# Attention, routed experts and a gated layer on one core: the attention loop in one reordered form, embedding norms on GpSimd, gates in four parts, queries a tile sooner

## The chip, the cores and the metric

One core of a Trainium2 chip runs the whole program. The metric is the device time of one execution in microseconds (us), lower is better. PE is TensorE, DVE is VectorE, ACT is ScalarE, POOL is GpSimd, SP is SyncE, which issues most of the DMAs.

## The reference

Three layers, one after the other: a gated linear attention with a state per head (4 batches, 8 heads, 768 steps, 40 channels), a layer of 8 experts of which each token takes the one with the largest logit, and a gated layer.

```python
for t in range(S):                                   # attention
    m_new = max(f_gate[t] + m, i_gate[t])
    f_stab, i_stab = exp(f_gate[t] + m - m_new), exp(i_gate[t] - m_new)
    C = f_stab * C + i_stab * outer(v[t], k[t])      # state, 40 x 40 per head
    n = f_stab * n + i_stab * k[t]
    y[t] = sigmoid(o_gate[t]) * (C @ q[t]) / max(abs(n . q[t]), 1)
x = y as 3072 tokens of 320 channels
logits = norm(x) @ norm(expert_emb).T / tau          # experts
out[mask_e] = softmax weight * (relu(x @ w1[e]) @ w2[e])
return (sigmoid(x @ w_gate) * (x @ w_val)) @ w_out   # gated layer
```

## The kernel before

The sequence is cut into 6 chunks of 128 steps, with 4 batches: 24 tiles, numbered i, chunk c = i // 4 and batch b = i % 4. Inside a tile the attention is a masked matrix product; between the chunks of a batch a state cst[b] is carried. The code is written in the order in which each engine gets its instructions (no scheduler moves them), and each engine works its list strictly in that order. So a step that waits holds all that stands behind it on the same engine.

The steps of one tile, with the line of the profile:

- `load_qk`, `load_kv` (L283, L288): SP's DMAs of queries and keys (six buffers) and of keys, values and output gates (five buffers).
- `st_S(i)` (L422): PE multiplies keys and queries into two PSUM banks (s_ps). DVE masks the first half into am (L441), ACT copies it to f16 as ah (L442); DVE masks the second half in place (L443), ACT copies it (L444); POOL subtracts al for the first half (L445), DVE al for the second half (L446). ah and al are the high and low part of one number.
- `st_V(i)`, `st_V2(i)`: POOL scales the values into vw (L409), ACT copies vh (L418), POOL subtracts vl (L419).
- `st_AV(i)` (L449): PE multiplies state with queries and ah, al with vh, vl into o_ps, always bank 4 in the loop.
- `post_ops(i)` (L492): three small DVE operations on den, the sigmoid of the output gate on ACT (L490), x0 on DVE (L518), then POOL's `gated`: x (L504) and a copy of its last 64 columns (L507).
- `st_U(i)` (L468): PE's update of the state into u_ps (bank 5), then cst[b]: two operations, one for each half of the heads; on ACT in chunk 0 (L483), on DVE later (L485).
- `st_XT(i)` (L525): PE transposes x, ACT copies it to xt (L531) and sums squares (L534), SP stores x to xs.
- `st_logit(i)` (L537): three small matmuls, and DVE's copy to raw, which the profile names rs (L545).
- `st_route(c)`, `st_rank(c)`: DVE's choice of the expert (rmax, sel), four small sums on POOL (run, L569), some small matmuls on PE, and nine DVE operations (pf, posf, bm, oh_p, ob, oh_b). Eight of the nine go to the list `sideq`, from which `side()` takes one at a time.

The gates are computed by six DVE operations over 32 lanes (`gate_ops`, two of them scans along the sequence) and two exps on ACT (`st_gexp`); `st_gates2` transposes them on PE. They come in three parts: chunk 0, chunk 1, and chunks 2 to 5 together (512 columns). ACT loads a function table whenever it changes between Exp and Sigmoid.

The order around the change is written by hand. Tiles 0 to 2 run in a prologue of their own, woven with 15 small DVE operations that normalise the expert embeddings (`emb_norm`, with `sqrt_ops`). Then a loop runs i from 3 to 19. One round of it holds: loads for tile i+4, XT(i-1), AV(i), post(i), U(i), the rank step in every fourth round, V2(i+1), S(i+3), V(i+2), logit(i-1), route in every fourth round. Tiles 20 to 23 follow in a tail that is woven with the first expert's weights; then come the experts and the gated layer, which the change leaves as they are.

Of the kernel before, what the change touches and what calls it, by code (L numbers as in the profile page):

```python
# [22 lines left out]
def kernel(  # L23
# [250 lines left out]
    def kpart(i):  # L274
        return kv[i % NKV][:, KO:VO].rearrange("p (h d) -> p h d", d=D)
# [28 lines left out]
    def emb_norm():  # L304
        esq = ap_.tile([NE, DM], F32, name="esq")
        en1 = ap_.tile([NE, 4], F32, name="en1")
        return [
            lambda: nc.scalar.activation(out=esq, in_=eb, func=AF.Square, accum_out=en1[:, 0:1])
        ] + sqrt_ops(ap_, en1[:, 1:2], en1[:, 0:1]) + [
            lambda: nc.vector.tensor_scalar(  # L310
                out=en1[:, 2:3], in0=en1[:, 1:2], scalar1=1e-6, scalar2=tb, op0=ALU.add, op1=ALU.mult
            ),
            lambda: nc.vector.reciprocal(en1[:, 3:4], en1[:, 2:3]),
            lambda: nc.vector.tensor_scalar_mul(eb, eb, en1[:, 3:4]),
        ]
# [152 lines left out]
    def st_U(i):  # L468
# [68 lines left out]
    def st_logit(i):  # L537
# [7 lines left out]
        nc.vector.tensor_copy(raw[:, i, :], lp[:, 0:NE])  # L545
# [9 lines left out]
    def st_rank(c):  # L555
# [14 lines left out]
        pf = bp.tile([P, B, NE], F32, tag="pf", name="pf")  # L570
# [108 lines left out]
    NAHEAD = 3  # L679
    sideq = []  # L680
# [9 lines left out]
    st_S(0, lambda: st_gates2(0, 1))  # L690
    def load(i):
        load_qk(i)
        load_kv(i)

    post = {}

    def early(i):
# [16 lines left out]
    st_V(2)
    st_S(2, lambda: (early(0), st_V2(1)))
    load(4)
    st_U(0)
    st_V2(2)
    st_V(3)
    st_gates2(1, 2)  # L720
    load_qk(6)
    st_sig(0)
    st_sig(1)
    post[0][5]()
    st_S(3, lambda: early(1))
    st_U(1)
    st_V2(3)
    side(2)
    post[1][5]()
    load(5)  # L730
    st_S(4, lambda: (st_XT(0), early(2), side(len(sideq))))
    st_sig(2)
    load_kv(6)
    post[2][5]()
    st_V(4)
    st_U(2)
    st_S(5, lambda: (st_XT(1), emb_T(), st_AV(3), st_post(3)))
    sideq += gate_ops(2 * L, S)
    GX = 5
    for i in range(3, NTILE - B):  # L740
        load(i + 4)
        if i > 3:
            st_XT(i - 1)
            st_AV(i)
            post = post_ops(i)
            if i == GX + 1:
                del post[3]
            weave(post)
        else:
            st_logit(0)  # L750
            st_XT(2)
# [10 lines left out]
        st_U(i)  # L762
        if i > B and i % B == 1:
            rk = st_rank(i // B - 1)
            rk.pop(0)()
            sideq += rk
# [1312 lines left out]
```

## Time and profile before

| | us |
|---|---|
| three runs | 765.41, 765.99, 767.67 |
| median | 765.99 |
| the profiled execution, its own time | 767.39 |
| its span, first to last instruction | 765.6 |
| attention loop with its prologue, read from DVE | 0 to about 132 |
| PE busy in the span | 730.9 (95%) |
| DVE, ACT, POOL busy in the span | 402.4, 363.9, 395.5 |

The profile shows one execution. A row of a group gives line, engine, operation, output and inputs, their shapes, how often it ran, its busy time and the mean of one in ns, and the idle time of the engine just ahead of it with what ended that idle time. A row of a timeline gives start and length in us. The granted clock (PEclk) is 1.00 where TensorE runs at 2.4 GHz and 0.50 where it runs at 1.2 GHz.

### The profile page before, as it was taken

What the parts mean: (1) busy time and instruction counts of PE and PEld (TensorE: products, weight loads), DVE (VectorE), ACT (ScalarE), POOL (GpSimd) and SP (SyncE); (2) the same over time, 40 slices, a digit from 0 to 9 for tenths busy, and PEclk for the clock granted to TensorE, in tenths of its full rate; (3) what the DMA queues carried; (4) which work ended last, traced back from release to release, by engine and by line L of the source; (5) the groups of instructions that cost most, each with busy time, mean ns of one, the idle gap of its engine ahead of it and who ended that gap; (6) DMA issues with size and microseconds to landing.
All of it is one profiled execution on the core that took longest, in us unless ns stands there. A gap on an engine that the chain in (4) does not pass through costs nothing. (4 is left out here: it accounts for less than half of the span.)

```text
span 765.6 us, 17594 instructions
## 1 busy us (share of the span) xinstructions
PE 730.9 (95%) x6861; PEld 656.2 (86%) x6861; DVE 402.4 (53%) x864; ACT 363.9 (48%) x829; POOL 395.5 (52%) x449
## 2 busy tenths in 40 slices
PE   7789999899999999999989999999999999999995
PEld 6689998789888889999878888888888888888884
DVE  7878888778579787755576664223212111111111
ACT  5756554545775556666354454333323333333222
POOL 6667777647576767787153223544324334334222
PEclk9899999689999999999999999999999999999998
DMA  7644864544545565553122320000000000000001
GB/s 247 172 148 131 248 198 135 168 128 136 162 137 155 147 194 176 166 168 92 35 55 78 84 58 32 36 22 15 2 2 36 1 2 36 2 1 36 2 1 39
DMA packets 39864, 70.46 MB, mean 92 GB/s; under 512 B 4818, under 2 KB 28460, under 8 KB 39772
## 3 DMA queue, kind: packets, MB, share of 16 engines
q1 hardware_dynamic: 36764, 59.61, 26.1%
q0 software_dynamic: 3008, 9.64, 3.8%
q8 instruction: 56, 0.92, 0.5%
q14 instruction: 36, 0.29, 0.1%
HBM read 60.55 MB, written 8.68 MB: 90 GB/s over the span
## 5 line engine op out<-in xcount | busy, mean ns | idle before, releaser
L1586 POOL TENSOR_TENSOR hl<-sgm,hh 128x512 fp32r<-128x512 f32 x71 | 94.9, 1342 | 228.1 <-ACT hh L1585 228.1
L1575 DVE TENSOR_TENSOR sgm<-v_ps,sgm 128x512 f32<-128x512 f32 (+1 forms) x73 | 49.7, 682 | 229.8 <-ACT sgm L1574 229.8
L1611 PE MATMUL o_ps<-wo,hl 64*128 64x320 f32 x560 | 87.2, 307 | 0.0
L1610 PE MATMUL o_ps<-wo,hh 64*128 64x320 f32 x560 | 86.7, 305 | 0.0
L1609 PE MATMUL o_ps<-wo,hh 64*128 64x320 f32 x560 | 86.3, 303 | 0.0
L1574 ACT ACTIVATE sgm<-g_ps 128x512 f32<-128x512 f32 (+1 forms) x73 | 43.2, 593 | 76.8 <-PE g_ps L1533 76.8
L1545 ACT COPY seen<-zeros 1x1 f32<-1x1 f32 x142 | 27.0, 190 | 109.1 <-PE v_ps L1533 61.5
L1585 ACT CAST hh<-sgm 128x512 fp32r<-128x512 f32 (+1 forms) x73 | 44.8, 615 | 47.9 <-DVE sgm L1575 47.6
L1014 ACT ACTIVATE hh<-h_ps 128x256 fp32r<-128x256 f32 (+7 forms) x72 | 35.2, 489 | 57.8 <-PE h_ps L926 54.8
L1531 PE MATMUL v_ps<-xg,wvh 64*128 64x512 f32 x144 | 56.5, 392 | 2.4 <-ACT seen L1545 2.4
L429 PE MATMUL s_ps<-qk 128*128 128x128 f32 (+1 forms) x384 | 54.4, 305 | 4.2 <-DMA qk<-in_qkt_dram 4.1
L1609 PEld LDWEIGHTS o_ps<-wo,hh 64*128 64x128 f32 x560 | 53.0, 185 | 6.3
L1610 PEld LDWEIGHTS o_ps<-wo,hh 64*128 64x128 f32 x560 | 52.8, 184 | 5.8
L1531 PE MATMUL g_ps<-xg,wgh 64*128 64x512 f32 x144 | 56.5, 392 | 0.0
L1532 PE MATMUL v_ps<-xg,wvh 64*128 64x512 f32 x144 | 56.4, 392 | 0.0
L1532 PE MATMUL g_ps<-xg,wgh 64*128 64x512 f32 x144 | 56.4, 392 | 0.0
L1532 PE MATMUL g_ps<-xl,wgh 64*128 64x512 f32 x144 | 56.4, 392 | 0.0
L1532 PE MATMUL v_ps<-xl,wvh 64*128 64x512 f32 x144 | 56.4, 392 | 0.0
L1531 PE MATMUL g_ps<-xh,wgh 64*128 64x512 f32 x144 | 56.3, 391 | 0.0
L1531 PE MATMUL v_ps<-xh,wvh 64*128 64x512 f32 x144 | 56.3, 391 | 0.0
L1533 PE MATMUL g_ps<-xg,wgl 64*128 64x512 f32 x144 | 56.2, 390 | 0.0
L1533 PE MATMUL v_ps<-xg,wvl 64*128 64x512 f32 x144 | 56.2, 390 | 0.0
(350 smaller groups left out, 2617.9 us busy)
## 6 DMA issues: line engine op xcount, KB each, us to landing
kv<-in_kvo_dram SPq DMA_DIRECT2D x24, 484.0 KB
w2raw<-in_moe_w_dram SPq DMA_DIRECT2D x32, 320.0 KB
w1raw<-in_moe_w_dram SPq DMA_DIRECT2D x32, 256.0 KB
qk<-in_qkt_dram SPq DMA_DIRECT2D x48, 160.0 KB
xs<-x SPq DMA_DIRECT2D x24, 192.0 KB
w1raw<-in_moe_w_dram SPq DMA_DIRECT2D x64, 64.0 KB
raw<-in_moe_w_out_dram SPq DMA_DIRECT2D x12, 320.0 KB
raw<-in_moe_w_gate_dram SPq DMA_DIRECT2D x8, 384.0 KB
```

The lines of the kernel that those rows point to most:

```text
L429: nc.tensor.matmul(pss[u][:, pr_ * L:(pr_ + 1) * L], qk[i % NQ][rows, 2 * u, pr_, :], qk[i % NQ][rows, 1, pr_, :], start=True, stop=True,)
L1014: nc.scalar.activation(out=h[f][0], in_=ps, func=AF.Relu)
L1531: lambda: nc.tensor.matmul(ps, at(wh), h[rows, kk], start=start, stop=False),
L1532: lambda: nc.tensor.matmul(ps, at(wh), l[rows, kk], start=False, stop=False),
L1533: lambda: nc.tensor.matmul(ps, at(wl), h[rows, kk], start=False, stop=stop),
L1574: nc.scalar.activation(out=s[:, cs], in_=pg[:, cs], func=AF.Sigmoid)
L1575: nc.vector.tensor_tensor(out=s[:, cs], in0=pv[:, cs], in1=s[:, cs], op=ALU.mult)
L1585: nc.scalar.copy(gh[:, cs], s[:, cs])
L1586: e.tensor_tensor(out=gl[:, cs], in0=s[:, cs], in1=gh[:, cs], op=ALU.subtract)
L1609: lambda: nc.tensor.matmul(o, gh[rows, ts_], wh[rows], start=begin, stop=False),
L1610: lambda: nc.tensor.matmul(o, gh[rows, ts_], wl[rows], start=False, stop=False),
L1611: lambda: nc.tensor.matmul(o, gl[rows, ts_], wh[rows], start=False, stop=end),
```

## The change

- The loop runs from i = 0 to 19; the prologue keeps only S of tiles 0 to 2 and what they need. A round now holds: queries of tile i+5 and keys and values of tile i+4, AV(i), XT(i-1), V2(i+1), post(i), U(i), S(i+3) with logit(i-1) inside, the rank step after it, V(i+2).
- The state update becomes one DVE operation for all heads into cc[b] (104 lanes, of which 24 hold nothing of use; the even heads' matmul writes 64 rows instead of 40), and two ACT copies from cc to cst. It stands inside S(i+3), between DVE's second masking and its subtraction.
- The logit copy goes from DVE to ACT for tiles below 20.
- The embedding norm computes its inverse root on POOL, with two DVE operations at its start and one near its end.
- The gates come in four parts: chunk 0, 1, 2, and 3 to 5 (384 columns).
- S of nine tiles (8, 10, 11, 13, 14, 16, 17, 19, 20) multiplies only the 40 rows that hold data, at partitions 0 and 64, instead of 128 rows with zeros; before, only tile 0 did.

The diff, cut to its core (the removed prologue of before, most of it, is the first "..." in the loop's part):

```diff
@@ emb_norm
+        step = [
+            lambda: two(t, y, sq, y, ALU.mult, ALU.mult),
+            lambda: two(t, t, -0.5, 1.5, ALU.mult, ALU.add),
+            lambda: g.tensor_tensor(out=y, in0=t, in1=y, op=ALU.mult),
+        ]
...
+        ] + 3 * step + [
+            lambda: g.tensor_tensor(out=y, in0=y, in1=sq, op=ALU.mult),
+            lambda: two(t, y, 1e-6, tb, ALU.add, ALU.mult),
+            lambda: v.reciprocal(r, t),
+            lambda: g.tensor_scalar_mul(eb, eb, r),
         ]
@@ st_S
-    def st_S(i, then=None):
+    def st_S(i, then=None, last=None):
...
-            rows = slice(0, P) if i else slice(DP * u, DP * u + D)
+            rows = slice(DP * u, DP * u + D) if i == 0 or i in HALF else slice(0, P)
...
+        aA[i] = (ah, al)
+        if last:
+            last()
         nc.vector.tensor_tensor(out=al[:, 1], in0=ps[1], in1=ah[:, 1], op=ALU.subtract)
-        aA[i] = (ah, al)
@@ st_U
-        for u in range(2):
-            sl = slice(DP * u, DP * u + D)
...
+        def add():
+            sl = slice(0, DP + D)
             pv = pu[sl, 0:NPR * DV].rearrange("p (a d) -> p a d", a=NPR)
             if c == 0:
-                nc.scalar.activation(out=cst[b][sl, :, u], in_=pv, func=AF.Copy, scale=SQ)
-                continue
-            nc.vector.scalar_tensor_tensor(
-                out=cst[b][sl, :, u], in0=pv, scalar=SQ, in1=cst[b][sl, :, u], op0=ALU.mult, op1=ALU.add
-            )
+                nc.vector.tensor_scalar_mul(cc[b][sl], pv, SQ)
+            else:
+                nc.vector.scalar_tensor_tensor(
+                    out=cc[b][sl], in0=pv, scalar=SQ, in1=cc[b][sl], op0=ALU.mult, op1=ALU.add
+                )
+            for u in range(2):
+                sl = slice(DP * u, DP * u + D)
+                nc.scalar.copy(cst[b][sl, :, u], cc[b][sl])
+
+        return add
@@ st_logit
-        nc.vector.tensor_copy(raw[:, i, :], lp[:, 0:NE])
+        (nc.scalar.copy if i < NTILE - B else nc.vector.tensor_copy)(raw[:, i, :], lp[:, 0:NE])
@@ prologue and loop
+    HALF = [i for i in range(8, NTILE - B + 1) if i % 3]
...
+    st_S(0, None, lambda: (st_gates2(0, 1), weave(ahead[0:2])))
+    weave(ahead[2:])
     st_V(0)
     st_V2(0)
+    norm = emb_norm()
+    weave(norm[0:7])
     st_gexp(L, 2 * L)
     st_S(1)
+    act_zero(qk[0])
     st_V(1)
+    weave(norm[7:])
+    st_S(2)
+    load_qk(4)
...
+    for i in range(NTILE - B):
+        if i + 5 < NTILE:
+            load_qk(i + 5)
+        load_kv(i + 4)
+        st_AV(i)
+        if i:
             st_XT(i - 1)
-            st_AV(i)
...
+        st_V2(i + 1)
+        post = post_ops(i)
+        if i in (G2 + 1, G3):
+            del post[3]
+        weave(post)
+        weave(scans.get(i, []))
...
-        st_U(i)
...
+        add = st_U(i)
...
-        st_S(i + NAHEAD, (lambda: st_logit(1)) if i == 3 else None)
+        def between():
+            add()
+            if i == 1:
+                emb_T()
+            if i:
+                st_logit(i - 1)
+
+        st_S(i + NAHEAD, None, between)
+        if i > B and i % B == 1:
+            rk = st_rank(i // B - 1)
...
+        if i == G2:
+            st_sig(i + 1)
+            st_gexp(2 * L, 3 * L)
+        if i == G3 - 1:
+            st_sig(i + 1)
+            st_gexp(3 * L, S)
```

What stands in a row on DVE in one round of the middle of the loop, before. The names are the steps' outputs; ob, oh_p and bm belong to the rank step.

```order
L545 COPY rs<-l_ps 128x8
L510 TENSOR_TENSOR den<-o_ps,ri_all 128x8
L513 SCALAR_TENSOR_TENSOR den<-o_ps,den 128x8
L516 RECIPROCAL den<-den 128x8
L518 TENSOR_TENSOR x_1327<-o_ps,den 128x320
L580 TENSOR_SCALAR bm<-bm 128x4
L485 SCALAR_TENSOR_TENSOR cst_135<-u_ps,cst_135 40x4x41 x2
L583 SCALAR_TENSOR_TENSOR bm<-bm,posf 128x4
L586 TENSOR_TENSOR oh_p<-iota_p,bm 128x512
L441 TENSOR_TENSOR am<-s_ps,cmask 128x512
L443 TENSOR_TENSOR s_ps<-s_ps,cmask 128x512
L446 TENSOR_TENSOR al<-s_ps,ah 128x512
```

The same round on DVE in the changed kernel:

```order
L531 TENSOR_TENSOR den<-o_ps,ri_all 128x8
L534 SCALAR_TENSOR_TENSOR den<-o_ps,den 128x8
L537 RECIPROCAL den<-den 128x8
L539 TENSOR_TENSOR x_1450<-o_ps,den 128x320
L604 SCALAR_TENSOR_TENSOR bm<-bm,posf 128x4
L607 TENSOR_TENSOR oh_p<-iota_p,bm 128x512
L611 TENSOR_TENSOR ob<-blk,bm 128x128
L452 TENSOR_TENSOR am<-s_ps,cmask 128x512
L454 TENSOR_TENSOR s_ps<-s_ps,cmask 128x512
L501 SCALAR_TENSOR_TENSOR cc_140<-u_ps,cc_140 104x164
L460 TENSOR_TENSOR al<-s_ps,ah 128x512
```

The copy rs is gone, the two cst operations have left the stretch between x and am, and one cc stands between the second masking and al.

On POOL, one round before (vw of a tile, then x and its copy for the tile two ahead of it in the loop, then vl, then al):

```order
L409 TENSOR_TENSOR vw<-kv_131,w_all 128x328
L504 TENSOR_TENSOR x<-x_1025,kv_130 128x320
L507 COPY x<-x 128x64
L419 TENSOR_TENSOR vl<-vw,vh 128x328
L445 TENSOR_TENSOR al<-am,ah 128x512
```

and in the changed kernel:

```order
L420 TENSOR_TENSOR vw<-kv_132,w_all 128x328
L430 TENSOR_TENSOR vl<-vw,vh 128x328
L525 TENSOR_TENSOR x<-x_1135,kv_131 128x320
L528 COPY x<-x 128x64
L456 TENSOR_TENSOR al<-am,ah 128x512
```

vl has moved up to stand right behind vw.

On ACT, the rows around the last part's exps (it, ft) before; kv is the sigmoid of the output gate:

```order
L490 ACTIVATE kv_129<-kv_129 128x320
L378 ACT_TABLE_LOAD
L378 ACTIVATE it<-it 32x512
L379 ACTIVATE ft<-Gt 32x512
L531 COPY xt<-tp_x 128x384
L534 ACTIVATE jk,rs<-x 128x320
L418 CAST vh<-vw 128x328
L442 CAST ah<-am 128x512
L444 CAST ah<-s_ps 128x512
```

and in the changed kernel, where the same pattern stands once more, earlier, for chunk 2:

```order
L506 COPY cst_133<-cc_137 40x4x41 x2
L566 COPY rs<-l_ps 128x8
L511 ACTIVATE kv_132<-kv_132 128x320
L389 ACT_TABLE_LOAD
L389 ACTIVATE it<-it 32x384
L390 ACTIVATE ft<-Gt 32x384
L552 COPY xt<-tp_x 128x384
L555 ACTIVATE jk,rs<-x 128x320
L429 CAST vh<-vw 128x328
L453 CAST ah<-am 128x512
L455 CAST ah<-s_ps 128x512
```

The copies cst and rs have come to ACT, and one pair of table loads (to Exp and back) more stands in its list.

## Rows read from the trace of the kernel before

**Rows 1.** The page: busy time by engine; granted clock in 40 slices, tenths.

```profile
PE 730.9 (95%) x6861; PEld 656.2 (86%) x6861; DVE 402.4 (53%) x864; ACT 363.9 (48%) x829; POOL 395.5 (52%) x449
PEclk9899999689999999999999999999999999999998
```

**Rows 2.** Stretches: busy us (instructions) PE, PEld, DVE, ACT, POOL; clock; DMA share; GB/s.

```profile
60.00:80.00 20.00, 18.74 (x288) 18.09 (x287) 16.84 (x53) 11.00 (x26) 14.88 (x24) 1.00 0.51 155
...
140.00:160.00 20.00, 19.38 (x143) 18.93 (x143) 14.67 (x48) 9.31 (x26) 11.33 (x18) 0.54 0.42 122
```

**Rows 3.** Groups on DVE, 57 to 131 us: busy us, mean ns | idle before.

```profile
L446 DVE TENSOR_TENSOR al<-s_ps,ah 128x512 f16<-128x512 f32 x13 | 9.0, 691 | 8.5 <-ACT ah L444 8.5
...
L485 DVE SCALAR_TENSOR_TENSOR cst<-u_ps,cst 40x164 f32<-40x164 f32 x26 | 8.4, 322 | 0.2
...
L545 DVE COPY rs<-l_ps 128x8 f32<-128x8 f32 x13 | 2.0, 155 | 0.0
```

**Rows 4.** Timeline on DVE: am of tiles 2, 6, 18, 19 and 22.

```profile
18.50 0.67 DVE L441 TENSOR_TENSOR am<-s_ps,cmask 128x512 f32<-128x512 f32 x1
...
39.74 0.68 DVE L441 TENSOR_TENSOR am<-s_ps,cmask 128x512 f32<-128x512 f32 x1
...
106.26 0.69 DVE L441 TENSOR_TENSOR am<-s_ps,cmask 128x512 f32<-128x512 f32 x1
...
110.68 0.69 DVE L441 TENSOR_TENSOR am<-s_ps,cmask 128x512 f32<-128x512 f32 x1
...
131.44 0.68 DVE L441 TENSOR_TENSOR am<-s_ps,cmask 128x512 f32<-128x512 f32 x1
```

**Rows 5.** Groups on POOL, 57 to 131 us.

```profile
L445 POOL TENSOR_TENSOR al<-am,ah 128x512 f16<-128x512 f32 x13 | 15.1, 1159 | 6.1 <-ACT ah L442 6.1
L504 POOL TENSOR_TENSOR x<-x,kv 128x320 f32<-128x320 f32 x14 | 12.4, 884 | 10.4 <-ACT vh L418 8.4 <-issue 1.0 <-ACT kv L490 1.0
L419 POOL TENSOR_TENSOR vl<-vw,vh 128x328 f16<-128x328 f32 x15 | 12.1, 810 | 1.3 <-ACT vh L418 1.3
L409 POOL TENSOR_TENSOR vw<-kv,w_all 128x328 f32<-128x328 f32 x14 | 10.3, 736 | 0.2 <-DVE w_all L389 0.2
L507 POOL COPY x<-x 128x64 f32<-128x64 f32 x14 | 4.8, 344 | 0.9
L569 POOL TENSOR_TENSOR run<-run,sel 128x8 bf16<-128x8 bf16 x12 | 2.4, 198 | 0.7
```

**Rows 6.** Timeline on POOL: the vl that stands directly behind its vw.

```profile
12.73 0.81 POOL L419 TENSOR_TENSOR vl<-vw,vh 128x328 f16<-128x328 f32 x1 [0.57 <-ACT vh L418]
```

**Rows 7.** Timeline on ACT: a pair of cst copies; a table load and its successor.

```profile
25.96 0.61 ACT L483 ACTIVATE cst<-u_ps 40x164 f32<-40x164 f32 x2
...
60.35 1.28 ACT L490 ACT_TABLE_LOAD   x1
61.64 0.47 ACT L490 ACTIVATE kv<-kv 128x320 f32<-128x320 f32 x1
```

**Rows 8.** Timeline on PE: S with 40 rows; S with 128; transposes of two rounds.

```profile
4.63 2.07 PE L429 MATMUL s_ps<-qk 40*128 40x128 f32 x14
...
35.31 3.74 PE L429 MATMUL s_ps<-qk 128*128 128x128 f32 x16
...
40.14 0.52 PE L529 MATMUL tp_x<-ident,x 128*128 128x128 f32 x3
...
42.49 2.05 PE L429 MATMUL s_ps<-qk 128*128 128x128 f32 x16
...
44.97 0.44 PE L529 MATMUL tp_x<-ident,x 128*128 128x128 f32 x2
```

**Rows 9.** Stretches of 2 us, columns as in rows 2.

```profile
30.00:32.00 2.00, 0.40 (x16) 0.29 (x12) 1.35 (x5) 1.96 (x6) 1.43 (x2) 1.00 0.62 213
32.00:34.00 2.00, 1.51 (x7) 1.51 (x8) 1.83 (x6) 1.59 (x5) 1.94 (x4) 0.51 0.89 296
...
134.00:136.00 2.00, 0.81 (x6) 0.74 (x6) 1.70 (x8) 0.90 (x4) 1.98 (x4) 1.00 1.02 350
```

More of the change, by code (lines that the diff above doesn't have):

```diff
@@ L272 @@
     cst = [bp.tile([P, NPR, 2, DV], F32, name=f"cst{b}", bufs=1) for b in range(B)]
-    def kpart(i):
-        return kv[i % NKV][:, KO:VO].rearrange("p (h d) -> p h d", d=D)
+    cc = [bp.tile([P, NPR, DV], F32, name=f"cc{b}", bufs=1) for b in range(B)]
     def vpart(i):
@@ L306, in emb_norm @@
         en1 = ap_.tile([NE, 4], F32, name="en1")
+        sq, y, t, r = (en1[:, j:j + 1] for j in range(4))
+        yi = y.bitcast(I32)
+        v, g = nc.vector, nc.gpsimd
+        two = lambda o, x, a, b, op0, op1: g.tensor_scalar(out=o, in0=x, scalar1=a, scalar2=b, op0=op0, op1=op1)
+        step = [
[3 more added lines that the diff above has]
+        ]
         return [
[L308 to L311, printed above, removed]
-            ),
-            lambda: nc.vector.reciprocal(en1[:, 3:4], en1[:, 2:3]),
-            lambda: nc.vector.tensor_scalar_mul(eb, eb, en1[:, 3:4]),
+            lambda: nc.scalar.activation(out=esq, in_=eb, func=AF.Square, accum_out=sq),
+            lambda: v.tensor_single_scalar(out=yi, in_=sq.bitcast(I32), scalar=1, op=ALU.logical_shift_right),
+            lambda: v.tensor_scalar(
+                out=yi, in0=yi, scalar1=-1.0, scalar2=float(0x5F3759DF), op0=ALU.mult, op1=ALU.add
+            ),
+        ] + 3 * step + [
[3 more added lines that the diff above has]
+            lambda: g.tensor_scalar_mul(eb, eb, r),
         ]
@@ L382, in st_gates2 @@
         n = (hi - lo) * BH
-        tp = bank(5, "tp_r") if lo > 1 else tp_ps("tp_r")
+        tp = tp_ps("tp_r")
         for u, src in ((0, aexp), (1, rexp)):
@@ L569, in st_rank @@
             nc.gpsimd.tensor_tensor(out=run, in0=run, in1=sl[:, b, :], op=ALU.add)
-        pf = bp.tile([P, B, NE], F32, tag="pf", name="pf")
+        pf = bp.tile([P, B, NE], F32, tag="pf", name="pf", bufs=1)
         bm = bp.tile([P, 2, B], F32, tag="bm", name="bm")
@@ L685, in side @@
                 sideq.pop(0)()
+    ahead = gate_ops(L, 2 * L)
     for op in gate_ops(0, L):
@@ L689 @@
     st_gexp(0, L)
[L690 to L697, printed above, removed]
-        st_AV(i)
-        post[i] = post_ops(i)
-        weave(post[i][0:3] + post[i][4:5], [side] * 4)
-    sideq += gate_ops(L, 2 * L)
+    st_S(0, None, lambda: (st_gates2(0, 1), weave(ahead[0:2])))
+    weave(ahead[2:])
     st_V(0)
-    side(6)
     st_V2(0)
-    sideq += emb_norm()
-    side(1)
-    act_zero(qk[0])
+    norm = emb_norm()
+    weave(norm[0:7])
     st_gexp(L, 2 * L)
     st_S(1)
+    act_zero(qk[0])
     st_V(1)
[L714 to L742, printed above, removed]
-            st_XT(i - 1)
[L744 to L751, printed above, removed]
+    weave(norm[7:])
+    st_S(2)
+    load_qk(4)
+    G2, G3 = 3, 9
+    third, others = gate_ops(2 * L, 3 * L), gate_ops(3 * L, S)
+    scans = {i: third[2 * i:2 * i + 2] for i in range(G2)}
+    scans.update({G2 + j: others[j:j + 1] for j in range(len(others))})
+    for i in range(NTILE - B):
[4 more added lines that the diff above has]
+        if i:
+            st_XT(i - 1)
+        st_V2(i + 1)
[4 more added lines that the diff above has]
+        weave(scans.get(i, []))
         side(1 + (i > 16))
@@ L761 @@
                 load_w2(0, p)
-        st_U(i)
[L763 to L766, printed above, removed]
+        add = st_U(i)
         side(1 + (i > 16))
-        st_V2(i + 1)
-        if i > GX:
-            side(1 + (i > 16))
+        side(1 + (i > 16))
         if i == NTILE - B - 1:
@@ L776 @@
             load_x(0)
-        st_S(i + NAHEAD, (lambda: st_logit(1)) if i == 3 else None)
-        if i == GX + 1:
-            st_gates2(2, NCH)
+        def between():
[7 more added lines that the diff above has]
+            rk = st_rank(i // B - 1)
+            rk.pop(0)()
+            sideq += rk
+        if i == 0:
+            st_gates2(1, 2)
+        if i == G2 + 1:
+            st_gates2(2, 3)
+        if i == G3:
+            st_gates2(3, NCH)
         if i < NTILE - B - 1:
             st_V(i + 2)
-        if i == GX:
-            st_sig(GX + 1)
-            st_gexp(2 * L, S)
+        if i == G2:
[4 more added lines that the diff above has]
+            st_gexp(3 * L, S)
         if i == 8:
             no_places()
-        st_logit(i - 1)
-        if i % B == 0:
+        if i and i % B == 0:
             st_route(i // B - 1)
```

4 lines of the change are left out of this document (3 added, 1 removed).

## The prediction

> **What bounds the kernel now.** I read the page first, then the stages, then in the attention stage one engine after the other. The page says PE 95% busy [rows 1], but that is an average over stages with different limits: from about 160 us on the experts and the gated layer keep PE full, and no line of the change touches them. The attention loop runs before that. In the stretch from 60 to 80 us [rows 2] PE is busy 18.74 of 20 us, DVE 16.84, POOL 14.88 and ACT 11.00, so no busy share names the limit. The waits do. On DVE the groups of the stretch show almost no idle time except one: before the last subtraction of a tile (al, L446) it waits 8.5 us in 13 tiles, 0.65 each, for ACT's copy ah of what DVE itself has just masked [rows 3]. So DVE's order of work sets the round: its operations one behind the other, plus one hole of 0.65 us. The first masking of a tile (am) is the clock to read rounds from: tile 6 at 39.74 us, tile 22 at 131.44 [rows 4], 91.7 us in 16 rounds, 5.73 each. The other engines have room in 5.73: PE's own round, transpose to transpose, is 4.83 (40.14 to 44.97) [rows 8]; POOL's operations sum to 1.16+0.88+0.81+0.74+0.34+0.18 (four run adds per four tiles) = 4.11 [rows 5]; ACT's to 11.00/20 x 5.73 = 3.15 [rows 2].
>
> **DVE in the loop.** Before, the state update cst is two operations of 40 lanes behind x0: 8.4 us for 26, 0.65 per tile [rows 3]. Now it is one operation cc over 104 lanes with the same 164 columns. By its column count it should take what one of the two took, 0.32. It stands between ps1's masking and al, that is in the hole of 0.65, and al still waits for ah. So the whole 0.65 leaves the round. If lanes cost time after all (no row has this shape with 104), 0.32 could become up to 0.69, as the 128-lane al with 512 columns does [rows 3]; then 0.05 of it would stick out of the hole, which is the other bound and nothing. The logit copy (L545, 0.155 us alone) goes to ACT; neighbours overlap, so I count 0.1. Together 0.75 x 16 rounds = **-12.0 us**, to 79.7, or 4.98 per round. The two cst copies and the logit copy land on ACT: 0.61 for a pair [rows 7] and about 0.2, so ACT's round is 3.15+0.81 = 3.96, still under 4.98. What they hide behind is ACT's wait for the next am; the next reader of cst is four tiles later.
>
> **POOL becomes the next limit.** Its order changes from vw, x, copy, vl to vw, vl, x, copy. vl needs ACT's vh, which needs the vw just made; before, x stood in that time, now POOL waits it out. The one place in the trace with this order shows the wait: 0.57 [rows 6]. POOL's round is then 4.11+0.57 = 4.68. It is a floor under DVE's round. DVE's rounds are uneven: a tile without routing, rank or gate operations takes 4.42 (106.26 to 110.68) [rows 4], so 3.67 after the change, and the average 4.98 contains 1.31 of such operations. Rounds with few of them are lifted to 4.68. I take 6 of the 16, near 4.3, lifted by 0.35: **+2.0** (bounds: 0 if POOL's lateness is caught up in the heavy rounds, +5 if all light rounds sit at 5.0).
>
> **PE.** S of the nine tiles in HALF uses 40 rows at partitions 0 and 64 instead of 128. The only such rows are tile 0's, at 1.2 GHz: 13 steps in 2.07-0.42 us, 0.127 each, against 15 steps in 3.74-0.42, 0.22 each, for 128 rows at the same clock (the 0.42 is the length of the last one) [rows 8]. Ratio 0.58, so S falls from 2.05 to about 1.2 and PE's round from 4.83 to 4.0. This is off the path and counts as nothing. The reverse wait: U writes bank 5, which add now reads one step later, behind ps1. The ring add, U, S, am is about 1.56 (am to the end of add) + 0.45 + 2.05 = 4.1 for 128 rows, under 4.68. The rank matmuls move behind S, so S no longer stands behind a wait for sel; DVE's list covered that wait, I count nothing.
>
> **Gates in four parts, tables.** The scans keep their columns (512 become 128+384), so DVE's sum stays within 0.5 us. Each part needs Exp and then Sigmoid again, two more table loads of 1.28 us [rows 7], and more exps, for which I allow 0.5 each, a little over a cst copy. ACT has 4.98-3.96 = 1.0 us of room per round. The rounds with Exp take about 1.28+1.0 more, so ACT runs about 1.2 late twice. DVE waits for that at al, POOL at vh. I take **+1.5** (0 to 3). In the trace the load ends at 61.63 and the next ACT operation starts at 61.64 [rows 7]. The Trainium skill (ScalarE: Activation LUTs, What ACT_TABLE_LOAD costs) adds a drain of about 1.38 us to each switch, 2.66 in all. By that page two more switches would cost 2.8 us more, and the sum below would be -7.2; the row shows no such gap, so the rows' value stands.
>
> **The start.** Before, DVE also did 15 small operations of the embedding norm between tiles 1 and 5, and am went from 18.50 (tile 2) to 39.74 (tile 6) [rows 4], 5.3 a round. The last of these rounds is long because PE ran at 1.2 GHz: S took 3.74 [rows 8]. Now the norm is on POOL, ahead of al of tiles 1 and 2; DVE's reciprocal (r) stands ahead of am of tile 2 and waits for POOL's seven small operations, so tile 2 comes no earlier. From there four rounds at 4.7 to 5.0 reach tile 6 at about 38: **-1.5** (from -4 if PE stays at 2.4 GHz, to +2 if it falls again as at 32). SP: queries of i+5 are asked for one tile sooner; they wait for AV of i-1, which is done by then, and keys and values behind them in the queue wait for POOL's x as before. Nothing counted.
>
> **Sum.** -12.0+2.0+1.5-1.5 = -10.0 us. The tail after the loop is the same code, 10 us sooner. The profiled execution took 767.39 (span 765.6); -10.0 gives 757.4. The median of the three runs is 765.99, 1.4 lower, so **756.0**.
>
> **Rivals.**
> 1. *POOL is held up by DVE* (0.17). POOL's 128x64 copy is 0.24 us in most tiles but averages 0.344 [rows 5], so something stretches it. If half of the 1.31 us per round of DVE's side operations held POOL for their length, POOL's round would be 4.68-0.10+0.65 = 5.23 and the loop would save 16 x (5.73-5.23) = 8, with tables and start as above 758; with three quarters of them 5.56, 2.7 and 763. About 761. Against: vw and al of POOL vary little. The Trainium skill (SBUF — State Buffer, Who interferes with whom) says that a DVE instruction with two SBUF inputs contends with a GpSimd instruction that reads SBUF.
> 2. *PE falls to its lower clock inside the loop, slower* (0.09). Twice in the trace PE's clock fell to 1.2 GHz after a thin stretch: 0.40 us busy from 30 to 32, then 0.51 granted [rows 9]; 0.81 from 134 to 136, then most of 140 to 160 at 0.54 [rows 2, 9]. The 40-row S and a shorter list leave PE thinner in the loop. At 1.2 GHz S takes 3.74/2.05 = 1.82 times as long, a 40-row round about 7.3 and a full one 8.8, 2.3 to 3.8 over 4.98. From four such rounds on all is lost; six cost 18: 774. Against: between 40 and 132 us, where the loop of before runs, the page's slices show the clock at full [rows 1].
> 3. *The hole doesn't carry the add* (0.05), because add waits for U or PE's ring is longer than I count: DVE's round stays near 5.6, 764 to 767, no change.
> 4. *The tail keeps its clock* (0.09). If DVE's lead keeps PE fed at 134, the slice from 140 to 160 runs at 2.4 GHz; DVE was busy 14.67 of it [rows 2], so at most 5 us go: 751, and 745 with the best start.
>
> **The numbers.** The forecast itself has 0.60, with 750 to 761 from the bounds above. Leaving out 3 and most of 2, and the best ends of 4, the range is **745 to 764**. 0.3% is 2.3 us, about what a measurement of this kernel can tell from no change. Faster by more: 0.60+0.17+0.09 less 0.01 for the upper end of rival 1 = 0.85; within: 0.06; slower: 0.09.
>
> **What would show it.** DVE's idle time before al falls from 0.65 to about 0.3 with cc in front of it; am to am averages 4.9 to 5.1 from tile 6 to 22; POOL's vl shows a wait for vh near 0.57; copies cst and rs stand on ACT; am of tile 6 lies near 38 and of tile 22 near 121. Wrong would be: granted clock of 0.5 between 40 and 120 us, POOL idle under 0.2 per round with am rounds over 5.3, PE waiting for add before U, or a hole that stays at 0.65 with cc outside it.

## The result, and the profile after

The changed kernel took 772.23 us (median of 4 runs, 771.83 to 774.30) against 766.03 for the kernel before beside it: ratio 1.0078, 95% interval 1.0060 to 1.0095. It is **slower by 6.2 us**, where 10 us less had been forecast. The profiled execution took 771.83 with a span of 770.1 us, 4.5 more than the 765.6 of before. In what follows the logit copy on VectorE has executions in two groups (764 to 770 us and 775 to 778) with its profile from the upper one, and the last experiment has two of ten at 779 and 783, so that their medians say little.

The page of the changed kernel, answering to [rows 1]: busy time by engine, and the granted clock in 40 slices.

```profile
PE 731.4 (95%) x6861; PEld 655.9 (85%) x6861; DVE 396.1 (51%) x828; ACT 380.3 (49%) x885; POOL 398.4 (52%) x461
PEclk9799889799999999999999999999999999999998
```

PE's busy time is the same to 0.5 us. The line of the clock is not: it has eights in the fifth and sixth of its 40 slices (77 to 115.5 us), inside the attention loop, where before had nines. The stretches, answering to [rows 2], columns as there:

```profile
60.00:80.00 20.00, 15.47 (x229) 13.83 (x228) 15.44 (x38) 14.50 (x38) 13.70 (x20) 0.95 0.49 149
80.00:100.00 20.00, 20.00 (x291) 18.58 (x291) 13.96 (x40) 14.21 (x36) 13.46 (x22) 0.87 0.62 187
100.00:120.00 20.00, 19.20 (x263) 17.94 (x262) 13.59 (x38) 12.72 (x34) 13.97 (x23) 0.83 0.61 183
140.00:160.00 20.00, 15.86 (x155) 14.85 (x152) 16.16 (x42) 12.63 (x35) 13.30 (x18) 0.74 0.50 161
```

From 60 to 80 us PE is busy 15.47 us where it was busy 18.74, and in the two stretches after it the clock averages 0.87 and 0.83 where it was full. The tail stretch, in turn, rose from 0.54 to 0.74. The clock to read rounds from is again am on DVE, answering to [rows 4]; these are tiles 6, 12, 13, 14, 15, 17, 18 and 22.

```profile
41.86 0.65 DVE L452 TENSOR_TENSOR am<-s_ps,cmask 128x512 f32<-128x512 f32 x1
...
74.95 0.68 DVE L452 TENSOR_TENSOR am<-s_ps,cmask 128x512 f32<-128x512 f32 x1
...
85.87 0.69 DVE L452 TENSOR_TENSOR am<-s_ps,cmask 128x512 f32<-128x512 f32 x1 [1.52 <-PE s_ps L440]
91.14 0.68 DVE L452 TENSOR_TENSOR am<-s_ps,cmask 128x512 f32<-128x512 f32 x1
95.28 0.69 DVE L452 TENSOR_TENSOR am<-s_ps,cmask 128x512 f32<-128x512 f32 x1
...
105.12 0.69 DVE L452 TENSOR_TENSOR am<-s_ps,cmask 128x512 f32<-128x512 f32 x1 [0.63 <-PE s_ps L440]
113.16 0.69 DVE L452 TENSOR_TENSOR am<-s_ps,cmask 128x512 f32<-128x512 f32 x1 [2.33 <-PE s_ps L440]
...
136.45 0.68 DVE L452 TENSOR_TENSOR am<-s_ps,cmask 128x512 f32<-128x512 f32 x1
```

Tile 6 comes 2.1 us later than before, tile 22 5.0 later; what follows takes 0.5 less. So 2.1 us went in the start and 2.9 in the loop, whose 16 rounds take 94.6 in place of 91.7. Round n is the time from am of tile n to am of tile n+1. Half of the rounds are shorter than the 5.73 of before on average (round 14 takes 4.14), but round 12 takes 10.92 and round 17 takes 8.04 (5.73 and 5.23 before), and both end with DVE waiting for PE's S. The state update on DVE did what it should; DVE's groups from 57 to 131 us, answering to [rows 3]:

```profile
L460 DVE TENSOR_TENSOR al<-s_ps,ah 128x512 f16<-128x512 f32 x13 | 9.0, 692 | 6.9 <-ACT ah L455 6.9
...
L501 DVE SCALAR_TENSOR_TENSOR cc<-u_ps,cc 104x164 f32<-104x164 f32 x13 | 4.1, 315 | 0.0
```

One cc of 0.315 us on 104 lanes stands where two cst of 0.322 stood. The hole before al fell to 0.42 us in a plain round; the 6.9 us left hold one of 1.8, behind a table load.

The round of 10.92 us, on PE (start, length, what, wait before it):

```profile
72.79 2.05 PE L440 MATMUL s_ps<-qk 128*128 128x128 f32 x16
76.43 0.83 PE L562 MATMUL l_ps<-enT,xt 128*128 128x8 f32 x6 [1.58 <-ACT xt L552]
79.00 0.52 PE L398 MATMUL tp_r<-ident,it 32*128 32x32 f32 x3 [1.61 <-ACT rs L566]
...
79.78 2.00 PE L469 MATMUL o_ps<-cst,qk 128*128 128x82 f32 x8
```

and on ACT in the same time:

```profile
73.79 1.28 ACT L389 ACT_TABLE_LOAD   x1
75.08 0.52 ACT L389 ACTIVATE it<-it 32x384 f32<-32x384 f32 x1
75.51 0.51 ACT L390 ACTIVATE ft<-Gt 32x384 f32<-32x384 f32 x1
75.92 0.45 ACT L552 COPY xt<-tp_x 128x384 f32<-128x384 f32 x1
...
78.78 0.17 ACT L566 COPY rs<-l_ps 128x8 f32<-128x8 f32 x1
```

The Exps of the fourth gate part and their table load stand ahead of xt, for which the logit matmul waits. The logit copy rs, which the change moved to this queue, stands further back, and the gate transposes wait for the PSUM bank that it frees. The granted clock meanwhile (columns as in rows 2):

```profile
74.00:76.00 2.00, 0.84 (x8) 0.65 (x6) 1.83 (x6) 1.99 (x4) 0.01 (x1) 1.00 0.24 50
76.00:78.00 2.00, 0.97 (x11) 0.87 (x11) 0.47 (x2) 2.00 (x7) 0.73 (x1) 1.00 0.94 278
78.00:80.00 2.00, 0.99 (x7) 0.93 (x8) 0.90 (x3) 0.92 (x4) 1.94 (x4) 0.55 0.78 284
80.00:82.00 2.00, 2.00 (x20) 2.00 (x21) 0.31 (x2) 0.00 (x0) 1.74 (x6) 0.50 0.99 292
```

PE is busy less than half of the time from 74 to 80 us, and from 78 on it has 1.2 GHz, where AV's part on cst takes 2.00 us in place of 1.10.

### The profile page after: what moved, and what is told of

Read it like the earlier page. It is cut to its first block, busy times and chain, and to the rows that moved or that the text cites. A ratio compares the mean times of both kernels' runs of the same rounds, so it can differ in the third digit from the quotient of the medians.

```text
span 770.1 us, 17629 instructions
## 1 busy us (share of the span) xinstructions
PE 731.4 (95%) x6861; PEld 655.9 (85%) x6861; DVE 396.1 (51%) x828; ACT 380.3 (49%) x885; POOL 398.4 (52%) x461
## 5 line engine op out<-in xcount | busy, mean ns | idle before, releaser
L1612 PEld LDWEIGHTS o_ps<-wo,hh 64*128 64x128 f32 x560 | 53.8, 186 | 6.1
L1613 PEld LDWEIGHTS o_ps<-wo,hh 64*128 64x128 f32 x560 | 53.6, 185 | 5.7
L1536 PE MATMUL v_ps<-xh,wvl 64*128 64x512 f32 x144 | 56.2, 390 | 0.0
```

Source lines behind the costliest of these rows:

```text
L1536: lambda: nc.tensor.matmul(ps, at(wl), h[rows, kk], start=False, stop=stop),
L1612: lambda: nc.tensor.matmul(o, gh[rows, ts_], wh[rows], start=begin, stop=False),
L1613: lambda: nc.tensor.matmul(o, gh[rows, ts_], wl[rows], start=False, stop=False),
```

## Experiments

Theory A held the 40-row S guilty, B the fourth gate part with its table loads, C the start. Each run was compared with the kernel before on the same chip; "am 6 to 22" is the loop as above (91.7 before, 94.6 changed). Rounds, waits and clocks are those of the one profiled execution of each kernel, and executions of one kernel can lie 10 us apart.

**S on all rows, and three gate parts, one at a time and together.**

```
-    HALF = [i for i in range(8, NTILE - B + 1) if i % 3]
+    HALF = []
```

```
-    G2, G3 = 3, 9
-    third, others = gate_ops(2 * L, 3 * L), gate_ops(3 * L, S)
...
+    GX = 5
+    third = gate_ops(2 * L, S)
+    scans = {j: third[j:j + 1] for j in range(len(third))}
...
+            st_gexp(2 * L, S)
```

> The changed kernel with S on all 128 rows in every tile but tile 0 (the list of tiles with 40 rows is empty); nothing else differs. Theory A, the 40-row S leaves TensorE at the lower granted clock: the stretches at 1.2 GHz at 78.3 to 85.1 us and 105.6 to 112.4 us are gone, rounds 12 and 17 fall from 10.92 and 8.04 us to 5.5 to 6.0 each, am of tile 22 comes at about 129 instead of 136.5, time 763 to 767. Theory B, the gate part with its table load in tile 8's round holds TensorE up and the clock falls by that: the first stretch stays, the second goes at most, time 768 to 772. Theory C, the start and the stretched VectorE operations carry the loss and the clock is beside the point: time 771 to 773.

> The changed kernel with gates in three parts: the scans of 640 columns one a round in tiles 0 to 5, one pair of Exps with its table loads in tile 5, its transposes in tile 6, as the kernel before has them; the 40-row list stays. Theory B (gates and table load of tile 8 open the first stretch at the lower clock): that stretch is gone and round 12 is 5 to 6 us; time 765 to 768. Theory A (40-row S): both stretches stay somewhere between 60 and 115 us; time 770 to 773.

> Both edits: S on all rows and gates in three parts, the rest as changed. Theory A: no lower clock between 45 and 125 us, time within 1.5 us of the kernel with full rows alone (762 to 767). Theory B: 3 us or more under the kernel with full rows alone. If reordered loop, add in the hole and logit copy on ScalarE are worth what the forecast gave them (5 to 10 us), this one comes to 756 to 762.

Full rows alone: 774.25 us, ratio 1.0099 (1.0064 to 1.0133), round 12 still 11.6 with the clock low from 80 to 88; the second low stretch was gone, and another stood at 48 to 54. Three parts alone: 765.48, ratio 0.9991 (0.9955 to 1.0027), round 12 is 5.1, no low clock between 62 and 136 us, am 6 to 22 86.6. Both: 768.89, 1.0020 (0.9998 to 1.0042), am 6 to 22 88.4, not the 756 to 762 us that the forecast's terms for the loop would give. So A falls as the cause of round 12, and B holds: the interval of three parts lies below that of the changed kernel. What of the fourth part does it, the loads, the Exps, the scans or the transposes, is asked further down. With the gates in three parts the 40 rows look like a gain: 3.4 us by the medians, 2.2 by the ratios, whose intervals still overlap, and 2.8 in the rounds at full clock shown next.

**The two parts of the loop alone, in the kernel before.**

```
-            rows = slice(0, P) if i else slice(DP * u, DP * u + D)
+            rows = slice(DP * u, DP * u + D) if i == 0 or i in HALF else slice(0, P)
```

```
-        st_U(i)
+        add = st_U(i)
...
-        st_S(i + NAHEAD, (lambda: st_logit(1)) if i == 3 else None)
+        st_S(i + NAHEAD, (lambda: st_logit(1)) if i == 3 else None, add)
```

> The kernel before with one part of the change alone: S of tiles 8, 10, 11, 13, 14, 16, 17, 19 and 20 on 40 rows. Theory A: a new stretch at the lower granted clock inside the loop between 60 and 125 us, 2 to 8 us slower, 768 to 774. Theory B and C: no new stretch and 765 to 767.

> The kernel before with one part alone: U's sum kept in one buffer, one add on 104 rows standing ahead of al, and the two copies into cst on ScalarE; loop order, gates, start and full-row S as before (the working buffer of the route's product has one copy in place of two, for room). By the forecast's term (0.65 a round over 16 rounds) 755 to 758. By the theory that TensorE, at 5.07 us of work in a round with S on all rows, bounds the rounds anyway: am of tile 13 to am of tile 20 stays at 36 to 36.6 us and the time at 763 to 767.

> The kernel before with two parts: the add ahead of al (alone 767.2 against 766.4, no gain) and the 40-row S (alone 772.9, with lower clock in the loop). Theory of two bounds (VectorE's and TensorE's round both at 5.1 to 5.3 us, so that neither saves alone): rounds at the full clock between tiles 13 and 20 fall to 4.2 to 5.1 us and the time, where the clock holds, to 758 to 764. Theory that 40 rows lower the clock by themselves: stretches at the lower clock in the loop as with the 40 rows alone, 769 to 774.

The add in the hole alone: 767.19 us, ratio 1.0014 (1.0000 to 1.0029). That is no gain, where the forecast's term was 12 us less (with the logit copy). The 40 rows alone: 772.90, 1.0080 (1.0056 to 1.0104). Both: 772.76, 1.0071 (1.0044 to 1.0099), against the 758 to 764 that two equal bounds had let me expect. The stretch from 80 to 117 us shows how little room PE had; before, then with the add in the hole, then the new loop with three parts and full rows, then the same with 40 rows (columns as in rows 2):

```profile
80.00:117.00 37.00, 35.72 (x526) 34.16 (x526) 30.37 (x93) 19.99 (x49) 27.81 (x43) 1.00 0.71 214
```

```profile
80.00:117.00 37.00, 36.31 (x532) 35.66 (x531) 30.70 (x84) 24.67 (x64) 28.16 (x40) 1.00 0.75 224
```

```profile
80.00:117.00 37.00, 36.55 (x527) 34.96 (x525) 27.86 (x75) 25.45 (x70) 28.22 (x41) 1.00 0.73 220
```

```profile
80.00:117.00 37.00, 36.03 (x582) 33.56 (x577) 30.69 (x82) 28.46 (x79) 30.43 (x44) 1.00 0.78 238
```

PE was busy 35.72 of 37 us before, and is busy 36.55 in the new loop with full rows. am 13 to 20 takes 36.5, 36.1 and 36.2 us in the first three, and 33.4 in the last, where only S is shorter: in the new loop PE is the bound there. In the kernel before, on DVE:

```profile
80.10 0.69 DVE L441 TENSOR_TENSOR am<-s_ps,cmask 128x512 f32<-128x512 f32 x1
...
116.64 0.69 DVE L441 TENSOR_TENSOR am<-s_ps,cmask 128x512 f32<-128x512 f32 x1
```

On PE in the third kernel (new loop, full rows), S follows S in 5.07 us with no wait in between (the cut rows are AV's 24 small matmuls):

```profile
88.78 2.05 PE L440 MATMUL s_ps<-qk 128*128 128x128 f32 x16
90.67 0.73 PE L562 MATMUL l_ps<-enT,xt 128*128 128x8 f32 x6
91.26 1.10 PE L469 MATMUL o_ps<-cst,qk 128*128 128x82 f32 x8
...
92.80 0.52 PE L550 MATMUL tp_x<-ident,x 128*128 128x128 f32 x3
93.26 0.66 PE L490 MATMUL u_ps<-vw,kv 128*64 128x41 f32 x16
93.85 2.05 PE L440 MATMUL s_ps<-qk 128*128 128x128 f32 x16
```

In the order of before, PE is not the only bound. With the add alone, DVE's groups from 57 to 131 us show where the time that it saved went; first three groups of the kernel before, then the same three with the add in the hole:

```profile
L441 DVE TENSOR_TENSOR am<-s_ps,cmask 128x512 f32<-128x512 f32 x13 | 9.0, 691 | 0.3
...
L593 DVE TENSOR_TENSOR oh_b<-ob,tv 128x128 bf16<-128x128 f32 x4 | 1.3, 331 | 0.1
...
L577 DVE TENSOR_SCALAR bm<-posf 128x4 f32<-128x4 f32 x4 | 0.8, 209 | 0.1
```

```profile
L440 DVE TENSOR_TENSOR am<-s_ps,cmask 128x512 f32<-128x512 f32 x13 | 8.9, 685 | 2.1 <-PE s_ps L428 2.1
...
L602 DVE TENSOR_TENSOR oh_b<-ob,tv 128x128 bf16<-128x128 f32 x4 | 2.5, 625 | 0.1
...
L586 DVE TENSOR_SCALAR bm<-posf 128x4 f32<-128x4 f32 x4 | 2.2, 544 | 0.1
```

The state update fell from 8.4 to 4.1 us and the wait before al from 8.5 to 6.0, together 6.8 less. DVE's waits for PE (before am and den) rose by 3.3, and seven operations of the rank step, which are the same in both kernels, from 9.8 to 14.6. So the saving was lost again, in part as waiting for PE and in larger part as longer DVE operations; why these grew is not shown. Adding the 40 rows does not free these rounds either: in that kernel rounds 15 to 19, nearly all at the full clock, take 5.4, 5.6, 5.2, 3.7 and 5.9, where the theory of two bounds had 4.2 to 5.1, and PE is busy only 18.56 of 20 us from 97 to 117.

The 40 rows come with a lower clock in both orders. In the order of before, alone, five low stretches stand between 50 and 130 us. In the new loop with three parts one does, from 54 to 62, where round 8 takes 8.07 in place of 5.77 with full rows; with full rows the clock there is full. The four kernels further down with three parts and 40 rows have one too, between 54 and 66. With three parts and 40 rows:

```profile
54.00:56.00 2.00, 0.60 (x3) 0.50 (x3) 1.40 (x7) 1.92 (x6) 1.76 (x5) 0.73 0.76 184
56.00:58.00 2.00, 2.00 (x21) 1.72 (x20) 1.00 (x4) 1.99 (x3) 0.84 (x2) 0.50 0.83 302
```

PE waits 1.48 us there for POOL's run and is busy 0.60 of 2 us, against 1.21 with full rows. From 62 on the clock stays full in the new loop and not in the order of before. Ahead of that, from 66 to 78 us at the full clock, PE is busy 0.83 of the time with the 40 rows in the order of before, 0.92 with add and 40 rows, and 0.98 in the new loop with three parts; but before itself shows 0.90 and keeps its clock, so the cause is not settled.

**How the fourth gate part holds PE.** The logit copy back to VectorE; the gate transposes back to U's bank; the Exps one place later on ScalarE; the scans earlier; and two of these together.

```
-        (nc.scalar.copy if i < NTILE - B else nc.vector.tensor_copy)(raw[:, i, :], lp[:, 0:NE])
+        nc.vector.tensor_copy(raw[:, i, :], lp[:, 0:NE])
```

> The changed kernel with the logit copy on VectorE in every tile, as before; all else changed. In the changed kernel TensorE waits 1.61 us at 79.0 us for ScalarE's logit copy before the transposes of the fourth gate part, behind a table load, two Exps and five other ScalarE operations, and round 12 takes 10.92 us. Theory B1, the queue of ScalarE with the logit copy in it is what holds TensorE: the wait falls under 0.3 us, round 12 to 6 to 8 us with no stretch at the lower clock at 78 to 85 us, time 765 to 769. Theory B2, the table load itself holds TensorE (the logit matmul waits 1.58 us for xt): round 12 stays over 9 us, time 771 to 775 (0.1 us a round on VectorE more).

```
-        tp = tp_ps("tp_r")
+        tp = bank(5, "tp_r") if lo > 1 else tp_ps("tp_r")
```

> The changed kernel with the gate transposes after the first on the PSUM bank of U, as before, in place of the rotating transpose banks; all else changed. Theory B1 (the transposes wait for a bank that the logit copy on ScalarE still holds): the 1.61 us wait at 79.0 us goes, round 12 falls to 6 to 8 us and the time to 765 to 769. Theory B2 (the table load): round 12 stays over 9 us, 771 to 774.

```
-        if i in (G2 + 1, G3):
-            del post[3]
         weave(post)
         weave(scans.get(i, []))
+        if i == G2 + 1:
+            st_gexp(2 * L, 3 * L)
+        if i == G3:
+            st_gexp(3 * L, S)
...
-        if i == G2:
-            st_sig(i + 1)
-            st_gexp(2 * L, 3 * L)
-        if i == G3 - 1:
-            st_sig(i + 1)
-            st_gexp(3 * L, S)
```

> The changed kernel with four gate parts, the Exps of parts three and four (and their table loads) one place later on ScalarE: behind the copy of xt, the squares and the copy of vh, and behind the round's own sigmoid, in the idle time of 2.1 us that ScalarE has there before ah. Theory B2 (the loads ahead of xt hold the logit matmul 1.58 us, vl 3.26 us and by them TensorE, whose clock then falls): the waits for xt go, round 12 falls from 10.92 to 5.5 to 7.5 us with no lower clock at 78 to 85 us, time 763 to 768. Rival (any table load in a late round opens the lower clock, wherever it stands): round 12 stays over 9 us, 770 to 774.

The bank alone: 773.63 us, ratio 1.0093 (1.0076 to 1.0110), round 12 still 9.6: the wait at the bank is gone, the wait for xt (1.59) is unchanged, and the clock is low from 80 to 102. The Exps later alone: 774.06, 1.0086 (1.0054 to 1.0118), round 12 still 10.5, and another low stretch at 124 to 136. Both misses, and the second shows why; PE in that kernel:

```profile
82.73 0.52 PE L398 MATMUL tp_r<-ident,it 32*128 32x32 f32 x3 [3.47 <-ACT rs L566]
```

The wait for xt is gone and the same Exps are now waited for at the logit copy's bank. The logit copy on VectorE is inconclusive: its ratio is 1.0015 (0.9976 to 1.0053). Its profile has no wait at the bank, a wait of 1.40 for xt and a round 12 of 9.7 us, but whether cutting this path alone can end the round stays open.

> The changed kernel, four gate parts, with two edits at once: the Exps later on ScalarE (in the idle time ahead of ah) and the gate transposes on U's bank. The first alone turned the 1.58 us wait for xt into a 3.47 us wait for the logit copy's bank; the second alone left the wait for xt. Theory B3 (the loads reach TensorE by two paths, and both must be cut): no wait over 0.8 us on TensorE in round 12 but that for the Exps, round 12 falls to 5.5 to 8 us, time 763 to 769. Theory D (VectorE's scans of the fourth part in rounds 8 to 11 leave TensorE thin before): the clock still falls at about 80 us, round 12 over 9 us, 770 to 774.

```
-    scans.update({G2 + j: others[j:j + 1] for j in range(len(others))})
+    scans.update({G2 + j: others[2 * j:2 * j + 2] for j in range(3)})
```

> The changed kernel with the six scan operations of the fourth gate part two a round in tiles 3 to 5 in place of one a round in tiles 3 to 8; Exps, table loads and transposes stay in their places. Theory D: rounds 9 to 11 fall from 6.3, 5.9 and 5.7 us to 4.5 to 5.3, TensorE's busy share ahead of 78 us rises from 0.72 to over 0.9, and round 12 falls under 8 us: 764 to 768. Theory B3: rounds 9 to 11 fall by 0.5 us each at most 1.5 in all, but round 12 stays over 9 us: 770 to 772.

Exps later and U's bank together: 769.43 us, ratio 1.0033 (1.0004 to 1.0063), am 6 to 22 88.2, and round 12 is 6.5. PE there:

```profile
76.73 0.37 PE L398 MATMUL tp_r<-ident,it 32*128 32x32 f32 x3 [1.31 <-ACT it L389]
...
77.44 1.12 PE L469 MATMUL o_ps<-cst,qk 128*128 128x82 f32 x8
```

PE waits only for the Exps themselves, AV's part on cst takes 1.12, and the clock is full from 54 to 136 us. The scans earlier: 770.58, 1.0032 (1.0004 to 1.0061); rounds 9 to 11 take 5.3, 4.0 and 4.8 where the changed kernel has 5.9, 5.7 and 4.3 (the 6.3, 5.9 and 5.7 of the text above are its rounds 8 to 10), but round 12 stayed at 9.7 with the clock low from 80 to 90, and both waits are still there (0.90 and 1.61).

By these traces the two paths make round 12: where one wait is cut the other stays and so does the round, and with both cut it is 6.5. The times do not show it as plainly. Both paths cut and the scans earlier gain alike (1.0033 and 1.0032, each spread over nearly 9 us), and neither is shown to reach three parts (0.9991). So the fourth gate part is shown as the cause by the time, the two paths by single executions. The second long round (17) had no run of its own. It follows a stretch in which PE waits 0.80 for POOL's run (1.20 busy from 102 to 104 us), with the clock low until 113; in every other trace of the new loop it takes 5.3 to 5.7, also where round 12 stays long, and its cause stays open.

**The start, and a better kernel.** From the kernel with three parts: the norm's steps on GpSimd moved behind S(2), its reciprocal and scaling into S(3); then the Exps later as well; then the steps on VectorE in place of GpSimd, or the gate transposes on U's bank.

```
-    weave(norm[7:])
     st_S(2)
+    weave(norm[7:14])
...
             add()
+            if i == 0:
+                weave(norm[14:])
```

> The kernel with three gate parts (40-row list kept) and the embedding norm later: its Newton steps on GpSimd stand behind the operations of S(2), its reciprocal on VectorE and the scaling behind the masks of S(3). In the kernel with three parts VectorE waits 2.83 us at 16.4 to 19.3 us for the steps on GpSimd, ahead of am of tile 2. Theory C, that wait is the loss of the start: am of tile 6 falls from 42.5 to 39.5 to 40.5, the stretch at the lower clock at 20 to 32 us shortens, time 761 to 764. Rival: the start is bound by other things, such as AV(1) behind the post operations of tile 0: am of tile 6 at 42 to 42.6, time 764 to 767.

> The kernel with three gate parts and the later norm, its Exps in the same later place (behind xt, squares, vh and sigmoid of tile 6). Theory B2: the stretch at the lower clock at 54 to 58 us goes and round 8 falls from 7.2 to about 5.5 us, time 1 to 2 us under the kernel with the later norm, 762 to 763. Rival: round 8 is held by GpSimd's four adds for the route (1.48 us wait of the transposes), nothing changes, 763.5 to 765.

> The same as the kernel with later norm and later Exps, with the norm's steps and the scaling on VectorE in the same places, none on GpSimd. Theory: GpSimd's steps at 18.7 to 21.6 us and 24.7 to 26.3 us hold vl(1) and vw by 3.0 and 1.6 us; on VectorE each costs 0.15 us, am of tile 6 falls from 40.0 to 38.5 to 39.5, time 760.5 to 762.5. Rival: am of tile 3 is pushed by VectorE's 2 us and nothing is won: 762.5 to 764.5.

> The kernel with three gate parts, later norm and later Exps, and now the gate transposes on U's bank. Theory B3: TensorE's gap at 55.0 to 55.7 us before the transposes goes at most in part (there it waits for the Exps themselves, 0.68 us), the lower clock at 56 to 62 us shortens or goes, 760.5 to 763. Rival: nothing changes, 762 to 764.

In the kernel with three parts DVE reads

```profile
19.34 0.15 DVE L324 RECIPROCAL en<-en 8x1 f32<-8x1 f32 x1 [2.83 <-POOL en L309]
19.42 0.66 DVE L452 TENSOR_TENSOR am<-s_ps,cmask 128x512 f32<-128x512 f32 x1
```

and with the norm later am of tile 2 is at

```profile
16.14 0.68 DVE L452 TENSOR_TENSOR am<-s_ps,cmask 128x512 f32<-128x512 f32 x1
```

Tile 2 comes 3.3 us sooner, tile 6 came at 39.99 instead of 42.54, and the time is 763.94 us, ratio 0.9955 (0.9933 to 0.9977). That is faster than the kernel before, but its interval and that of three parts (0.9955 to 1.0027) overlap, so the gain over three parts is likely and not shown. With the Exps later too: **763.12, ratio 0.9949 (0.9927 to 0.9972)**, the best kernel of the study, 0.5% faster than before and faster than the changed kernel; it is not told apart from the one without the later Exps. Its theory missed: the low stretch at 54 to 58 us did not go but stands at 56 to 62, and round 9 takes 7.5.

The norm on VectorE gave 764.71 (0.9973, 0.9944 to 1.0002): am of tile 1 came 1.0 us later and am of tile 3 2.7, so its rival came true in the trace, though the times of the two places do not differ clearly. U's bank on top gave 765.89 (0.9965, 0.9930 to 1.0001), no gain shown. That kernel has the same start as the best one, yet its tile 6 comes at 43.0 against 38.5: tile 6 varies by that much between executions, with the length of the low stretch before it, so the 2.6 us at tile 6 is weaker evidence than tiles 2 and 3 (16.1 to 16.9 and 20.9 to 21.7 in the three kernels with this start, 19.4 and 24.2 in the one with three parts).

## Why the prediction was wrong

By the profiled executions (before, changed, three parts) the sum of the text stands against this: loop edits -5.1, fourth gate part +8.0, start +2.1, what follows -0.5, together the +4.5 between the spans.

**DVE's term, -12.0: the edit right, its price wrong.** cc took 0.315, stood in the hole, and al's wait fell to 0.42. The failed step is the price of 0.75 us times 16 rounds, with PE "off the path" and counted as nothing, and with DVE's other operations taken to keep their lengths. The add alone brought nothing (1.0014): of DVE's saving 3.3 us came back as waits for PE and 4.8 as longer rank operations. The 5.73 of before is a mean over unlike rounds. Before, am 13 to 20 takes 36.5 us (tiles 18 and 19 in [rows 4] lie in it), 5.22 a round, and a round of PE with full rows is 5.07 in the new loop. Where PE bounds, only 0.15 was to be had. PE's 4.83, read from one pair of transposes [rows 8], was too short: U with its wider matmuls alone adds 0.15 (0.66 for 0.51), and 35.72 busy of 37 us in that stretch would have warned. The 60 to 80 us stretch that I read [rows 2] has PE at 0.94 and hid it. Rounds 6 to 12, where PE was busy 36.2 of 40 us, gained nothing from the add either (40.4 before, 40.8 with it), and what holds them is not shown. All loop edits together with three parts gave 3.3 us with full rows and 5.1 with 40 rows, by am 6 to 22, in place of the 10 of the terms for DVE and POOL.

**The 40 rows, 0.** The length was right (at full clock, in the changed kernel):

```profile
50.92 1.16 PE L440 MATMUL s_ps<-qk 40*128 40x128 f32 x16
```

Counting it as nothing was wrong in both directions. It shortens the engine that bounds rounds 13 to 20 of the new loop, and was worth 2.8 us there with three parts, 1.8 over am 6 to 22, where it also has the low stretch in round 8. In the order of before, where PE then ran thinner, it cost 5.7 us (ratio 1.0080).

**POOL's floor, +2.0.** The wait of vl for vh is there (0.57 in plain rounds) but no floor: rounds of 4.1 and 4.2 us occur in the changed kernel and with three parts. Rival 1 had DVE hold POOL up. What is seen is both longer where they meet: DVE's ob took 0.90 us beside a vl of 1.30 (means before 0.459 and 0.810).

```profile
63.51 1.30 POOL L430 TENSOR_TENSOR vl<-vw,vh 128x328 f16<-128x328 f32 x1 [0.57 <-ACT vh L429]
```

```profile
64.06 0.90 DVE L611 TENSOR_TENSOR ob<-blk,bm 128x128 f32<-128x128 f32 x1
```

The Trainium skill (SBUF — State Buffer, Who interferes with whom) says that a DVE operation with two SBUF inputs contends with a GpSimd operation that reads SBUF; these two rows agree. Whether all of the longer rank operations above come from that is not shown.

**Gates and tables, +1.5: measured +6.7.** That is the changed kernel (1.0078) against three parts (0.9991), and 8.0 in am 6 to 22 of the profiled executions. The failed step is "ACT runs about 1.2 late twice": I asked who waits on ACT and named DVE and POOL, not PE. In the traces PE waits by two paths, xt (1.58) and the bank behind the logit copy (1.61), and then runs at 1.2 GHz from 78 to 85 us. The price of a single load was right: it took 1.28 us and the Exp behind it began 0.01 later, so the drain that the Trainium skill (ScalarE: Activation LUTs, What ACT_TABLE_LOAD costs) adds is again not in the rows; 2.8 us of it would have come nearer for a wrong reason.

**The start, -1.5: measured +2.1.** The text itself saw that the reciprocal stands ahead of am of tile 2 and waits for POOL, and then counted no loss for it; moving it brought tile 2 forward by 3.3. The range named +2 for a fall of the clock, and the changed kernel has two low stretches there (22 to 32 and 34 to 38 us, against 32 to 40 before).

**The rivals.** Rival 2 (PE falls to the lower clock in the loop, slower, 0.09) is what happened, in two long rounds rather than six; it was given the 40 rows as its cause, which they are in the order of before, and not the fourth gate part, which it is for round 12 of the new loop. It had too small a chance: the text held against it that the loop of before keeps its clock, but the change was just what made PE thinner. Rival 4 came true in part, the tail's clock rose, and was worth 0.5 us. Two of the text's sums do not come out: with all bounds at their upper ends the forecast is 764 and not 761, and 745 needs the best end of every term, not of the start alone. Neither touches the result.

## What to carry to other kernels

Price an edit against each stretch's second bound, not against the mean round: put PE's busy time in that stretch beside the round before calling PE free, and look after the edit whether other operations of the engine grew. When an operation moves to another engine's queue, ask what its result frees (here a PSUM bank) and which long operation, a table load above all, can come to stand ahead of it. If a cut of one waiting path only moves the wait, look for the second path and cut both. Where executions differ by more than the effect, let the times of several decide and use one trace only to see where to look.

## What the runs showed of the hardware

Lanes cost nothing in these rows of VectorE: 104 lanes by 164 columns took 0.315 us, 40 lanes by 164 0.322. S on 40 rows in place of 128, with 16 matmuls, takes 1.16 us for 2.05 at the full clock, and U with 64 output rows in some of its matmuls 0.66 for 0.51. Seven small operations on GpSimd (8x1) took 2.05 us in a row, 0.18 to 0.33 each, and moving them out from between two tiles brought tile 2 forward by 3.3 us. Small operations on VectorE grew with an edit that leaves them as they are: bm (128x4) took 0.209 us on average in the kernel before and 0.544 with the add in the hole, oh_b (128x128) 0.331 and 0.625.
